# Scores tied behind the first MoE's matmuls, maxima in other PSUM banks, and one step less of lag, in a fused attention and two-MoE kernel

## The chip, the cores and the metric

The kernel runs on one core of a Trainium2 chip. The metric is the device time of one execution in microseconds (us), as a median over runs. Five engines work side by side, each on its own queue of instructions in a fixed order: TensorE (PE in the profile, its weight loads PEld), VectorE (DVE), ScalarE (ACT), GpSimd (POOL) and SyncE (SP), which here issues nearly all DMAs. The order in each queue is fixed when the program is built: a scheduler walks the instructions as they were written down, keeps a simulated clock, and gives each engine, whenever it is free on that clock, the earliest written instruction whose inputs and buffers are ready. On the chip an engine then works through its queue in that order and waits where an input is late.

## The reference, cut to what matters

```python
# attention: batch 4, heads 8, seq 576, head_dim 64
q_rot, k_rot = rotate(q), rotate(k)
scores = 1 / np.sqrt(D) * np.matmul(q_rot, k_rot.transpose(0, 1, 3, 2))
scores = scores - np.max(scores, axis=-1, keepdims=True)
attn = np.exp(scores)
attn = attn / (np.sum(attn, axis=-1, keepdims=True) + 1e-09)
x = np.matmul(attn, v)                       # then (B * S, H * D) = (2304, 512)
# first MoE: d_model 512, d_ff 768
h = np.maximum(np.maximum(x @ w1, x @ w2), x @ w3)
y = h @ w_out
# second MoE: d_model 512, d_ff 2048
h = y @ w_in
return (h * (1 / (1 + np.exp(-h)))) @ w_out2
```

## The kernel before, in words

**The attention** is cut into 80 tiles (`tiles`, filled from `order`, line 580). Four batches follow each other; each batch has a first part of its queries (256 columns, tiles 0 and 1 of each of four pairs of heads, 8 tiles in all) and a second part (320 columns, tiles 2, 3 and 4, 12 tiles; tile 4 is half as wide and takes both heads at once). Counted from 0, batch 1 is tiles 20 to 39, batch 2 tiles 40 to 59, batch 3 tiles 60 to 79. `attention()` (line 607) is a generator that writes down one step for each tile. In step j it writes the scores of tile j (`tile_scores`, lines 416, 417, 423 and 426, into the one tile `s` of three PSUM banks), their row maxima (`tile_max`, DVE, line 436) and exponentials (ACT, line 443). Then it writes later work on earlier tiles: the division of tile j-1 by its sums (`tile_norm`, ACT, line 455), and for batches 1 to 3 (`moved(b)`) a DMA that moves its 32-row blocks (`tile_move`, SP, line 494); for tile j-2 a transposition of the last columns through TensorE (`tile_last`, line 505; `turn_last`, lines 461 and 462); for tile j-3 a 32x32 transposition on DVE of what the DMA brought (`tile_flip`, line 516); then attention times V for a finished part of a pair (`av`, lines 557 and 561, its result read by ACT, line 564, and DVE, line 565). `av_at` says at which step a part's `av` is written: the index after its last tile plus 2, plus 1 for batches 1 to 3.

**The first MoE** runs inside the attention. Its work is cut into groups: an up group is 12 matmuls of one output block for one of w1, w2, w3, a down group 18 (`group`, line 640, matmuls on line 649). A batch has 36 up groups (18 on 256 columns for the first part, 18 on 320 for the second) and 8 down groups. From batch 1 on the first three up groups of the second part are written ahead of the first part's down groups. An up group's result is read by ACT (line 665, for w1) or by DVE (line 667, for w2 and w3), a down group's by ACT (line 691). While the attention lasts, groups write into `ps_m`, a ring of two PSUM banks, so the third group needs the first one's bank to be read. After each step the main loop at the end of `fused_kernel` gives groups out: `debt` grows by `RATE`, 8,000 columns, up to 24,000, and groups are written as long as it is positive, a group costing its columns times its matmuls (3,072 or 3,840 for an up group), and as long as the step has reached `x_ready` of the group's batch and part. So two or three up groups stand between two steps, none where the next part's x isn't there yet. With `x_ready[1, 1]` at 45 and `x_ready[2, 1]` at 65, steps 42 to 44 and step 64 give out none. Batch 3's groups start with one a step from step 77 on, and the rest follows when the attention is over, with five more banks (`ps_g`) in place of the attention's.

**Maxima over partitions** scale the fp16 pairs into which weights and activations are split. `all_max_a` (line 120 on PE, 122 on DVE) turns a column of maxima on TensorE and reduces it, `all_max_b` (line 128) spreads the result over the partitions, and `scale_of` (from line 143) reads it. Each takes a bank from `max_bank()` (line 114): a bank of `ps_m`, the ring of the groups. After tile 26 these are the maxima of V for batches 2 and 3, of `w_in` and of the second `w_out`.

**The turns.** `ps_t`, a ring of two banks with the tag `tr`, holds what TensorE transposes for the attention: q and k (`qk_turn`, lines 373 and 387) and the last columns of each tile (lines 461, 462 and 505).

**Beside all this** the weights of the second MoE are prepared (ACT lines 153, 227, 921, DVE lines 238, 239, 925, POOL lines 229 and 917, DMAs of SP), and after the attention come the rest of batch 3 and the second MoE (lines 1044 to 1139).

`tc.issue_after(x)` makes what is written inside it stand behind instruction `x` in the queue of x's engine. It sets the order alone and adds no wait.

Of the kernel before, what the change touches and what calls it, by code (L numbers as in the profile page):

```python
# [7 lines left out]
F32 = mybir.dt.float32  # L8
# [9 lines left out]
P = 128  # L18
# [4 lines left out]
def fused_kernel(  # L23
# [22 lines left out]
    nc = tc.nc  # L46
    B, H, S, D = q.shape
    NP = H // 2
# [26 lines left out]
    ps_m = Ring(ctx, "ps_m", 2, space=PSUM)  # L75
# [19 lines left out]
    ps_t = Ring(attn_pools, "ps_t", 2, space=PSUM)  # L95
# [13 lines left out]
    zscr = {nm: dram.tile([P, KC * (F2 // 512) * 512], F32, name="z" + nm) for nm in ("wi", "wo")}  # L109


    ps_am = []

    def max_bank():
        return (ps_am[0] if ps_am else ps_m).tile([P, 512], F32, tag="m", name="m")

    def all_max_a(m, ps=None):

        ps = ps or max_bank()
        nc.tensor.transpose(ps[0:1, 0:P], m, ident)  # L120
        t = small.tile([1, 1], F32, tag="amax", name="amax")
        nc.vector.tensor_reduce(out=t, in_=ps[0:1, 0:P], op=ALU.max, axis=AX.X)
        return t
# [147 lines left out]
    last = {}  # L271
# [87 lines left out]
    def moved(b):  # L359
        return b > 0  # L360
# [45 lines left out]
    def both(s, o, step, n):  # L406

        return bass.AP(tensor=s.tensor, offset=s.offset + o, ap=[list(s.ap[0]), [step, 2], [1, n]])
    evacs = [0]

    def tile_scores(key):
        b, hp, t = key
        T, K, Q = T_t[b, hp]
        s = ps_s.tile([P, 1536], F32, tag="s", name="s")
        if t == 4:
            nc.tensor.matmul(s[:, 0:512], Q, T[:, 512:1024], start=True, stop=True)
            last["score"] = nc.tensor.matmul(s[:, 512:576], Q, T[:, 1024:1088], start=True, stop=True).ins
            s_t[key] = s
            return
        n = P  # L420
        qs = T[:, t * P:t * P + n]
        kt = T[:, 512:1024]
        nc.tensor.matmul(both(s, 512, 448, 64), qs, K, start=True, stop=True)
        for g, o in ((0, 0), (1, 1024)):
            r = slice(64 * g, 64 * g + 64)
            last["s"] = last["score"] = nc.tensor.matmul(s[:, o:o + 512], qs[r], kt[r], start=True, stop=True).ins  # L426
        s_t[key] = s
# [4 lines left out]
    def tile_max(key):  # L432
        s = s_t.pop(key)
        m = heads(key)
        nb = small.tile([P, 2], F32, tag="nb", name="nb")
        x = nc.vector.tensor_reduce(  # L436
            out=nb[:, 0:m], in_=both(s, 0, 960, 576) if m > 1 else s[:, 0:576], op=ALU.max, axis=AX.X, negate=True
        )
        last["max"] = x.ins
        e = e_p.tile([P, 1152], F32, tag="e", name="e")  # L440
        sm = small.tile([P, 2], F32, tag="sm", name="sm")
        for g in range(m):
            x = nc.scalar.activation(  # L443
                out=e[:, HK[g]], in_=s[:, SK[g]], func=AF.Exp, bias=nb[:, g:g + 1], accum_out=sm[:, g:g + 1]
            )
        exps.append(x.ins)
        e_t[key], sum_t[key] = e, sm

    def tile_norm(key):
        e, m = e_t[key], heads(key)  # L450
        r = small.tile([P, 2], F32, tag="rec", name="rec")
        nc.scalar.activation(out=r[:, 0:m], in_=sum_t.pop(key)[:, 0:m], func=AF.Copy, bias=1e-9)
        nc.vector.reciprocal(out=r[:, 0:m], in_=r[:, 0:m])  # L453
        for g in range(m):
            nc.scalar.activation(out=e[:, HK[g]], in_=e[:, HK[g]], func=AF.Copy, scale=r[:, g:g + 1])  # L455
# [12 lines left out]
    def pt_of(key):  # L468
        b, hp, t = key
        r = int(t > 1)  # L470
        if (b, hp, r) not in pt_t:
            pt_t[b, hp, r] = pt_p.tile([P, 9, PARTS[r][1]], F32, tag="pt", name="pt")
        return pt_t[b, hp, r], P * t - PARTS[r][0]

    def blocks(pt):

        w = pt.shape[2]
        f = pt.rearrange("p c w -> p (c w)")
        return f[:, 0:8 * w].rearrange("p (i c k) -> p i c k", c=8, k=32), f[:, 8 * w:9 * w]

    def tile_move(key):

        e = e_t[key]
        pt, o = pt_of(key)
        main, i = blocks(pt)[0], o // 32
        for j in range(4):
            r = slice(32 * j, 32 * j + 32)
            if key[2] == 4:
                of = e[:, 128 * j:128 * j + 128]
                to = main[r, i:i + 2].rearrange("p i (g c) k -> p (i g) (c k)", g=2)  # L490
            else:
                of = bass.AP(tensor=e.tensor, offset=e.offset + 128 * j, ap=[list(e.ap[0]), [640, 2], [1, 128]])
                to = main[r, i:i + 4].rearrange("p i (g c) k -> p i g (c k)", g=2)
            nc.sync.dma_start(out=to, in_=of)
# [15 lines left out]
    def tile_flip(key):  # L510

        pt, o = pt_of(key)
        n = 2 if key[2] == 4 else 4
        x = blocks(pt)[0][:, o // 32:o // 32 + n].rearrange("p i c k -> p (i c k)")
        with tc.issue_after(last["max"]):
            nc.vector.transpose(out=x, in_=x)  # L516
# [28 lines left out]
    def av(b, hp, r):  # L545
        if hp == 0 and r == 0:
            x_t[b] = x_p[b % 2].tile([P, NP * S], F32, tag="x", name="x").bitcast(F16).rearrange("p (a x s) -> p a x s", a=NP, x=2)
        pt, vv = pt_t.pop((b, hp, r)), v_t[b, hp]
        o, n = PARTS[r][:2]
        v4 = vv[:, 0:4, :].rearrange("p a x -> p (a x)").rearrange("p (h c d) -> p h c d", h=2, c=4)  # L550
        xp = ps_x.tile([P, 512], F32, tag="xp", name="xp")
        if moved(b):
            main, mixed = blocks(pt)
            turned = lambda c, g: main[:, :, c + 4 * g, :]
        else:
            mixed, turned = pt[:, 4, :], lambda c, g: pt[:, c + 5 * g, :]
        nc.tensor.matmul(xp[:, 0:n], vv[:, 4, :], mixed, start=True, stop=False)
        for c in range(4):
            for g in range(2):
                r = slice(64 * g, 64 * g + 64)  # L560
                nc.tensor.matmul(xp[r, 0:n], v4[:, g, c, :], turned(c, g), start=False, stop=(c == 3))  # L561
        xh, xl = x_t[b][:, hp, 0, o:o + n], x_t[b][:, hp, 1, o:o + n]
        sv = sv_t[b][0]
        nc.scalar.activation(out=xh, in_=xp[:, 0:n], func=AF.Copy, scale=sv)
        nc.vector.scalar_tensor_tensor(
            out=xl, in0=xp[:, 0:n], scalar=sv, in1=xh, op0=ALU.mult, op1=ALU.subtract
        )
# [5 lines left out]
    PARTS = [(0, 256, (0, 1)), (256, 320, (2, 3, 4))]  # L573
    order = [(b, hp, r) for b in range(B) for r in range(2) for hp in range(NP)]
    tiles, events, first, x_ready, av_at = [], {}, {}, {}, {}

    def at(j, f, *a):
        events.setdefault(j, []).append((f, a))

    for b, hp, r in order:  # L580
        first.setdefault((b, hp), len(tiles))
        tiles += [(b, hp, t) for t in PARTS[r][2]]
        av_at.setdefault(len(tiles) + 2 + moved(b), []).append((b, hp, r))
        x_ready[b, r] = len(tiles) + 4 + moved(b)
    for i, (b, hp) in enumerate(pairs):
        u = first[b, hp]
        if b > 1:
            j = first[b, 0] + 3 * hp - 7
# [10 lines left out]
    for b in range(1, B):  # L599
# [4 lines left out]
        at(u, v_scale, b)  # L604
        at(u + 1, v_scale_b, b)

    def attention():

        back = lambda j, n: tiles[j - n] if n <= j < len(tiles) + n else None
        for j in range(len(tiles) + 5):  # L610
            if j < len(tiles):
                tile_scores(tiles[j])
                tile_max(tiles[j])
            key = back(j, 3)
            if key and moved(key[0]):
                tile_flip(key)
            for a in av_at.pop(j, ()):
                av(*a)
            key = back(j, 1)
            if key:  # L620
                tile_norm(key)
                if moved(key[0]):
                    tile_move(key)
            key = back(j, 2)
            if key:
                (tile_last if moved(key[0]) else tile_turn)(key)
            for f, a in events.pop(j, ()):
                f(*a)
            yield
# [11 lines left out]
    def group(passes, n, ps=None, more=False):  # L641

        first = ps is None
        if first:
            wide_n[0] += 1
            ring, tag = (ps_g[0], "mg") if ps_g and wide_n[0] % 7 > 1 else (ps_m, "m")
            ps = ring.tile([P, 512], F32, tag=tag, name=tag)
        for i, (l, r) in enumerate(passes):
            nc.tensor.matmul(ps[:, 0:n], l, r, start=(first and i == 0), stop=(not more and i == len(passes) - 1))  # L649
        return ps  # L650

    def moe1(b, pools):
# [672 lines left out]
        pass  # L1325
    for _ in wprep4:
        pass
    attn_pools.close()
    tail = ExitStack()
    ps_g.append(Ring(tail, "ps_g", 5, space=PSUM))  # L1330
# [82 lines left out]
```

## Time and profile before

| | |
|---|---|
| three runs: median, lowest, highest | 1001.32, 1000.82, 1008.92 us |
| the profiled execution, its span | 1006.66 us, 1004.8 us |
| mean granted clock of TensorE | 0.969 of full speed |
| busy share: PE, DVE, ACT, POOL | 92%, 70%, 60%, 49% |
| tile 26 starts, tile 79 starts, last attention matmul ends | 194.6, 576.4, 597.0 us |

The profile is of one execution, and its times are us from the start of its span. The span is shorter than the execution by what lies around it, 1.9 us here. PE, DVE, ACT, POOL are the busy times of the engines; a granted clock of 1.00 is 2.4 GHz, one of 0.50 is 1.2 GHz. An arrow <- behind an idle time names what ended it.

### The profile page before, as it was taken

To read this page: it belongs to the slowest core of one execution; us is meant where nothing else is said; L and a number is where in the kernel's file an instruction comes from. 1 tells how busy PE (TensorE), PEld (TensorE's weight loads), DVE (VectorE), ACT (ScalarE), POOL (GpSimd) and SP (SyncE) were. 2 spreads that over 40 slices of the span, in tenths; PEclk is the share of its full clock that TensorE was granted. 3 is DMA by queue.
4 is the path that set the end of the run, shared out by engine and by line. 5 is a ranking of instruction groups with operands and counts; after the bars stand their busy time and mean duration, and the time that the engine had idled before them with its cause. 6 is when DMAs were issued, how large, how long until landed. Compare 5 with 4: busy or idle time off the path is not lost. (4 is left out here: it accounts for less than half of the span.)

```text
span 1004.8 us, 19162 instructions
## 1 busy us (share of the span) xinstructions
PE 922.8 (92%) x6802; PEld 674.3 (67%) x6802; DVE 698.6 (70%) x1231; ACT 604.4 (60%) x1381; POOL 490.9 (49%) x546
## 2 busy tenths in 40 slices
PE   4577999999999899998998989999998999999997
PEld 2344665555666556665655567788887888888886
DVE  5779877967578556897767546854778767856554
ACT  2888577757667656787867623653563544554442
POOL 5835594961455500633322205653678259255264
PEclk9798999999999899999998999999999999999999
DMA  6943135877788965789988846264454253333201
GB/s 150 295 118 104 34 100 120 190 143 161 165 180 191 183 107 96 203 225 228 215 212 188 205 115 212 72 189 147 134 188 132 74 174 102 114 122 125 66 1 42
DMA packets 185198, 146.29 MB, mean 146 GB/s; under 512 B 51216, under 2 KB 168720, under 8 KB 185104
## 3 DMA queue, kind: packets, MB, share of 16 engines
q1 hardware_dynamic: 183600, 144.36, 56.5%
q8 instruction: 54, 0.88, 0.4%
q10 hardware_dynamic: 1504, 0.72, 0.3%
q14 instruction: 40, 0.33, 0.1%
HBM read 90.51 MB, written 26.21 MB: 116 GB/s over the span
## 5 line engine op out<-in xcount | busy, mean ns | idle before, releaser
L649 PEld LDWEIGHTS <-w 128*128 128x128 f16 x1632 | 161.5, 100 | 70.7 <-issue 24.5
L649 PE MATMUL m<-x,w 128*128 128x256 f16 (+1 forms) x1388 | 195.4, 292 | 13.1 <-ACT t L665 6.0
L1139 PEld LDWEIGHTS <-g 128*128 128x128 f16 x1485 | 146.2, 98 | 17.6
L1076 PEld LDWEIGHTS <-w8s 128*128 128x128 f16 x1344 | 131.1, 98 | 16.1 <-issue 1.0
L436 DVE TENSOR_REDUCE nb<-s 128x2 f32<-128x1152 f32 (+1 forms) x80 | 98.7, 1233 | 42.0 <-PE s L426 38.1
L443 ACT ACTIVATE e<-s,nb 128x576 f32<-128x576 f32 x144 | 105.3, 737 | 35.2 <-DVE nb L436 33.0
L917 POOL TENSOR_TENSOR z<-z 128x128 f32<-128x128 f32 (+1 forms) x96 | 60.8, 652 | 127.7 <-DMA z<-zwi 49.4
L229 POOL TENSOR_SCALAR z<-z 128x256 uint16<-128x256 uint16 x64 | 52.9, 826 | 123.0 <-ACT z L227 77.7
L455 ACT ACTIVATE e<-e,rec 128x576 f32<-128x576 f32 x144 | 104.5, 768 | 12.9 <-DVE rec L453 12.4
L426 PE MATMUL s<-T 64*128 64x512 f32 x256 | 85.9, 707 | 0.0
L561 PE MATMUL xp<-pt,vd 128*64 128x256 f32 (+1 forms) x512 | 81.5, 416 | 2.7 <-DVE pt L516 2.7
L1090 POOL TENSOR_TENSOR z<-t 128x256 f32<-128x256 f32 x32 | 27.1, 847 | 89.0 <-DVE t L1082 54.0
L516 DVE STREAM_TRANSPOSE pt<-pt 128x1024 f32<-128x1024 f32 (+1 forms) x60 | 67.6, 1127 | 2.8 <-DMA pt<-e 2.8
L1028 DVE SCALAR_TENSOR_TENSOR g<-gsum,sg,g 128x1024 f16<-128x1024 f32 x36 | 49.1, 1372 | 23.5 <-ACT g L1027 23.1
L352 POOL TENSOR_TENSOR w<-qk,sin_sb 128x512 f32<-128x512 f32 (+2 forms) x44 | 45.0, 1044 | 40.7 <-DMA qk<-in_q_dram 37.5
L649 PE MATMUL m<-h,wo 128*128 128x256 f16 (+1 forms) x448 | 63.2, 291 | 0.0
L1027 ACT ACTIVATE g<-gsum,sg 128x1024 f16<-128x1024 f32 x36 | 40.9, 1143 | 36.5 <-POOL gsum L1023 36.5
L649 PEld LDWEIGHTS <-wo 128*128 128x128 f16 x512 | 50.3, 100 | 17.2 <-issue 2.7
L561 PEld LDWEIGHTS xp<-pt,vd 128*64 128x64 f32 x512 | 35.9, 136 | 37.6 <-issue 13.4
L239 DVE SCALAR_TENSOR_TENSOR z<-z,z 128x256 int32<-128x256 int32 x64 | 36.3, 567 | 20.2 <-POOL z L229 19.0
L667 DVE SCALAR_TENSOR_TENSOR t<-m,t 128x256 f32<-128x256 f32 (+1 forms) x82 | 36.8, 449 | 18.5 <-PE m L649 15.7
L1139 PE MATMUL c<-w,g 128*128 128x256 f16 x376 | 48.9, 277 | 0.0
(246 smaller groups left out, 1970.7 us busy)
## 6 DMA issues: line engine op xcount, KB each, us to landing
w8s<-w8scr SPq DMA_DIRECT2D x64, 448.0 KB, 4.4
pt<-e SPq DMA_DIRECT2D x192, 128.0 KB, 4.0
z<-in_moe_w_in_dram SPq DMA_DIRECT2D x32, 256.0 KB, 3.9
z<-in_moe_w_out_dram SPq DMA_DIRECT2D x32, 256.0 KB, 3.7
w<-in_moe_w_dram SPq DMA_DIRECT2D x6, 768.0 KB, 5.2
wo<-in_moe_w_dram SPq DMA_DIRECT2D x6, 768.0 KB, 4.6
qk<-in_q_dram SPq DMA_DIRECT2D x32, 128.0 KB, 3.2
vd<-in_v_dram SPq DMA_DIRECT2D x16, 256.0 KB, 3.1
```

What stands on the lines that cost most here:

```text
L229: nc.gpsimd.tensor_scalar(out=q[:, :, 2], in0=q[:, :, 1], scalar1=step, scalar2=off, op0=ALU.mult, op1=ALU.add)
L426: last["s"] = last["score"] = nc.tensor.matmul(s[:, o:o + 512], qs[r], kt[r], start=True, stop=True).ins
L436: x = nc.vector.tensor_reduce(out=nb[:, 0:m], in_=both(s, 0, 960, 576) if m > 1 else s[:, 0:576], op=ALU.max, axis=AX.X, negate=True)
L443: x = nc.scalar.activation(out=e[:, HK[g]], in_=s[:, SK[g]], func=AF.Exp, bias=nb[:, g:g + 1], accum_out=sm[:, g:g + 1])
L455: nc.scalar.activation(out=e[:, HK[g]], in_=e[:, HK[g]], func=AF.Copy, scale=r[:, g:g + 1])
L516: nc.vector.transpose(out=x, in_=x)
L561: nc.tensor.matmul(xp[r, 0:n], v4[:, g, c, :], turned(c, g), start=False, stop=(c == 3))
L649: nc.tensor.matmul(ps[:, 0:n], l, r, start=(first and i == 0), stop=(not more and i == len(passes) - 1))
L917: nc.gpsimd.tensor_tensor(out=z[:, o], in0=z[:, x], in1=z[:, y], op=op)
L1028: nc.vector.scalar_tensor_tensor(out=l, in0=x, scalar=sg_t[jb], in1=h, op0=ALU.mult, op1=ALU.subtract)
L1076: nc.tensor.matmul(o, l, r, start=(i == 0), stop=(i == len(passes) - 1))
L1139: x = nc.tensor.matmul(ps, l, r, start=first, stop=last_, skip_group_check=True)
```

## The change

There are three edits.

- `group` keeps its last matmul in `last["group"]`, and from step 26 on (`j > LOOSE`) `tile_scores` is written inside `tc.issue_after(last["group"])`: the three or two score matmuls of tile j stand in TensorE's queue behind every group that was given out before step j.
- From step 26 on until the attention and the preparations that follow it have been written, `max_bank()` takes its bank from `ps_t` (tag `tr`) instead of `ps_m`.
- For the second part of batch 3 the extra step falls away: `tile_flip` of its 12 tiles is written 2 steps behind the scores instead of 3, and `av` and `x_ready` come one step earlier.

```diff
--- before.py
+++ after.py
@@ -109,10 +109,11 @@
     zscr = {nm: dram.tile([P, KC * (F2 // 512) * 512], F32, name="z" + nm) for nm in ("wi", "wo")}
 
 
-    ps_am = []
+    ps_am, b_now = [], [0]
 
     def max_bank():
-        return (ps_am[0] if ps_am else ps_m).tile([P, 512], F32, tag="m", name="m")
+        ring, tag = (ps_am[0], "m") if ps_am else (ps_t, "tr") if b_now[0] else (ps_m, "m")
+        return ring.tile([P, 512], F32, tag=tag, name=tag)
 
     def all_max_a(m, ps=None):
 
@@ -580,8 +581,9 @@
     for b, hp, r in order:
         first.setdefault((b, hp), len(tiles))
         tiles += [(b, hp, t) for t in PARTS[r][2]]
-        av_at.setdefault(len(tiles) + 2 + moved(b), []).append((b, hp, r))
-        x_ready[b, r] = len(tiles) + 4 + moved(b)
+        lag = int(moved(b) and (b, r) != (B - 1, 1))
+        av_at.setdefault(len(tiles) + 2 + lag, []).append((b, hp, r))
+        x_ready[b, r] = len(tiles) + 4 + lag
     for i, (b, hp) in enumerate(pairs):
         u = first[b, hp]
         if b > 1:
@@ -604,16 +606,22 @@
         at(u, v_scale, b)
         at(u + 1, v_scale_b, b)
 
+    LOOSE = 25
+    LAST = [(B - 1, hp, t) for hp in range(NP) for t in PARTS[1][2]]
+
     def attention():
 
         back = lambda j, n: tiles[j - n] if n <= j < len(tiles) + n else None
         for j in range(len(tiles) + 5):
+            b_now[0] = int(j > LOOSE)
             if j < len(tiles):
-                tile_scores(tiles[j])
+                with tc.issue_after(last["group"]) if j > LOOSE else nullcontext():
+                    tile_scores(tiles[j])
                 tile_max(tiles[j])
-            key = back(j, 3)
-            if key and moved(key[0]):
-                tile_flip(key)
+            for n in (3, 2):
+                key = back(j, n)
+                if key and moved(key[0]) and n == 3 - (key in LAST):
+                    tile_flip(key)
             for a in av_at.pop(j, ()):
                 av(*a)
             key = back(j, 1)
@@ -646,7 +654,8 @@
             ring, tag = (ps_g[0], "mg") if ps_g and wide_n[0] % 7 > 1 else (ps_m, "m")
             ps = ring.tile([P, 512], F32, tag=tag, name=tag)
         for i, (l, r) in enumerate(passes):
-            nc.tensor.matmul(ps[:, 0:n], l, r, start=(first and i == 0), stop=(not more and i == len(passes) - 1))
+            x = nc.tensor.matmul(ps[:, 0:n], l, r, start=(first and i == 0), stop=(not more and i == len(passes) - 1))
+        last["group"] = x.ins
         return ps
 
     def moe1(b, pools):
@@ -1325,6 +1334,7 @@
         pass
     for _ in wprep4:
         pass
+    b_now[0] = 0
     attn_pools.close()
     tail = ExitStack()
     ps_g.append(Ring(tail, "ps_g", 5, space=PSUM))
```

## Rows read from the trace of the kernel before

**Rows 1.** The page: span, and the granted clock in 40 slices.

```profile
span 1004.8 us, 19162 instructions
PEclk9798999999999899999998999999999999999999
```

**Rows 2.** Busy time by stage: length, PE, PEld, DVE, ACT, POOL, clock, DMA.

```profile
194.50:333.00 138.50, 131.12 (x831) 82.23 (x831) 100.47 (x176) 90.88 (x262) 73.89 (x80) 0.96 0.82 172
333.00:439.00 106.00, 102.38 (x655) 64.92 (x654) 71.14 (x128) 71.86 (x192) 29.16 (x37) 0.97 0.75 153
439.00:577.00 138.00, 125.73 (x790) 77.62 (x791) 97.54 (x189) 102.20 (x282) 41.85 (x71) 0.96 0.89 210
577.00:612.00 35.00, 31.50 (x243) 23.70 (x243) 15.65 (x39) 10.26 (x28) 2.31 (x4) 0.95 0.61 183
612.00:1004.80 392.80, 382.58 (x3409) 333.94 (x3406) 262.63 (x434) 192.05 (x293) 218.27 (x230) 0.99 0.36 113
```

**Rows 3.** Who waited for whom, PE, 194.5 to 612: us in total, times, longest.

```profile
PE s L423 <- ACT e L443: 5.9, 6, 2.1
PE s L416 <- ACT e L443: 5.7, 2, 3.6
PE m L649 <- ACT t L665: 4.0, 5, 1.4
PE m L649 <- DVE t L667: 3.5, 1, 3.5
PE m L649 <- DVE swie L143: 0.2, 1, 0.2
```

**Rows 4.** Busy time by stage, line 649 alone: PE (x matmuls), PEld, clock, DMA.

```profile
0.00:194.50 194.50, 41.77 (x312) 29.82 (x312) 0.93 0.51 137
194.50:304.90 110.40, 57.66 (x420) 41.73 (x420) 0.95 0.79 167
304.90:332.50 27.60, 12.59 (x96) 9.47 (x96) 1.00 0.92 187
332.50:409.30 76.80, 43.94 (x306) 30.65 (x306) 0.96 0.72 125
```

**Rows 5.** Busy time by stage, all instructions: four stretches, columns as in rows 2.

```profile
304.90:332.50 27.60, 25.68 (x173) 16.39 (x173) 22.14 (x43) 20.72 (x61) 20.01 (x22) 1.00 0.92 187
409.30:438.90 29.60, 29.11 (x200) 19.57 (x198) 26.28 (x47) 25.41 (x72) 15.93 (x21) 1.00 0.85 231
341.90:348.70 6.80, 6.64 (x25) 3.79 (x26) 3.63 (x6) 5.13 (x16) 1.19 (x2) 0.50 0.94 178
529.70:536.40 6.70, 5.76 (x18) 3.39 (x19) 5.58 (x13) 5.52 (x17) 3.09 (x6) 0.50 0.76 126
```

**Rows 6.** Timeline: start, us, engine, line, operation, count [idle before <-releaser].

```profile
530.64 2.07 PE L416 MATMUL s<-T,qd 128*128 128x512 f32 x2 [3.60 <-ACT e L443]
...
548.14 3.42 PE L649 MATMUL m<-x,w 128*128 128x320 f16 x24
...
570.86 0.38 PE L423 MATMUL s<-kd,T 128*128 128x128 f32 x2
...
574.75 0.74 ACT L443 ACTIVATE e<-s,nb 128x576 f32<-128x576 f32 x1
...
576.39 1.02 PE L416 MATMUL s<-T,qd 128*128 128x512 f32 x2
```

**Rows 7.** Timeline, 582 to 588: the end of the attention.

```profile
585.42 1.25 DVE L516 STREAM_TRANSPOSE pt<-pt 128x1024 f32<-128x1024 f32 x1 [2.81 <-DMA pt<-e]
...
587.11 1.17 PE L649 MATMUL m<-x,w 128*128 128x256 f16 x7 [3.50 <-DVE t L667]
```

**Rows 8.** Timeline, 444 to 448: a maximum over partitions.

```profile
444.29 0.27 PE L120 MATMUL m<-ident,vm 128*1 128x128 f32 x1
...
445.80 0.27 DVE L122 TENSOR_REDUCE amax<-m 1x1 f32<-1x128 f32 x1
```

**Rows 9.** DMA issues of the page: KB each, us from issue to landing.

```profile
pt<-e SPq DMA_DIRECT2D x192, 128.0 KB, 4.0
```

## The prediction

> **What bounds the kernel now.** I read the page's span and clock line first, then the busy times by stage, then who waited for whom on TensorE, and last the matmuls of line 649 counted by stretch. From the scores of tile 26 at 194.5 us to the end of the attention TensorE is busy 131.1 of 138.5, 102.4 of 106.0, 125.7 of 138.0 and 31.5 of 35.0 us [rows 2]. It is the bound, and 26.8 us of this stage are its idle time. The granted clock is below full here too: 138.5 x 0.04 + 106 x 0.03 + 138 x 0.04 + 35 x 0.05 = 16.0 us of full-speed time [rows 2], the lower digits in the clock line of the page [rows 1]. The matmuls themselves stay the same in number and shape. So about 43 us are all that the tie and the bank edit can win or share out anew; after 612 us TensorE has 382.6 of 392.8 us of work [rows 2], which the change does not touch.
>
> Which waits are they? Scores that wait for the exponentials of the tile before, 5.9 + 5.7 = 11.6 us in 8 waits; groups that wait for their bank or input, 4.0 + 3.5 us [rows 3]; the rest is spread over turns and `av`. The longest score wait, 3.60 us, is followed by score matmuls of 2.07 us, where the same two take 1.02 us at full clock [rows 6]: the stretch behind it ran 6.7 us at 0.50, and 6.8 us at 0.50 stand behind the 2.1 us wait at tile 46 [rows 3, 5]. That is (6.7 + 6.8) / 2 = 6.75 us more.
>
> **The tie: what it changes in the order.** Counting by the planner (8,000 columns a step, 3,072 or 3,840 a group), 396 matmuls of groups have been given out before step 26: 288 of batch 0's first half and 60 + 24 + 24 of its second. TensorE had issued 312 when the scores of tile 26 began [rows 4]: 84 behind, seven groups. At tile 41 the count is 792 given out (all 576 of batch 0, 216 of batch 1) against 312 + 420 = 732: 60 behind. At tile 55 it is 1134 against 312 + 420 + 96 + 306 = 1134 [rows 4]: none. So from tile 26 to about 54, and again from 60 to 77 (48 behind at tile 73), the edit changes the queue; between 55 and 59 the order is already the tied one.
>
> **Its gain.** Where the scores waited for exponentials, groups stood behind them with their data ready: two groups of 320 columns last 3.42 us [rows 6], enough for 2.1 and nearly for 3.60 us. Tied, such groups stand in front. At most this wins all of 11.6 + 6.75 = 18.4 us; at least nothing, since the mean number of groups between two scores stays the same and a late exponential can meet a thin step. I take half, -9.2 us, because the order is fixed by a planned time: before, scores were placed as soon as the plan had the exponentials done, with no margin, and tied they can only come later relative to the groups.
>
> **Its cost.** The stock of 24 to 84 matmuls is gone. Steps 42 to 44 and 64 give out nothing. From tile 41 to 45 the stock did 96 matmuls, 12.59 of 25.68 us of work [rows 4, 5]; without them 13.1 us are left for four steps, 3.3 us each. A step cannot be shorter than the chain from scores to the end of the second exponential, 570.86 to 575.49, 4.6 us [rows 6]. So an empty step idles 1.3 us. At step 44 the next part's first groups already have most of their x, so I count 42, 43 and 64: +4.0 us (0 to 5.2). Then the banks: before, groups came in pairs, one for each of the two banks (24 in one row [rows 6]). Tied, the 15 steps from 26 on that give out 36 or more matmuls have a third group in front of the scores, which needs the first one's bank read by ACT or DVE, behind their exponentials or maxima. The longest wait for such a read by ACT was 1.4 us [rows 3]. I take one such wait, +1.4, since two groups in a row already run without one; the ends are 0 and 15 x 1.4 = 21 us. A scores matmul queued behind a waiting group also holds the maximum and exponentials of its tile, which is part of these 21. Tie in all: -9.2 + 4.0 + 1.4 = -3.8 us.
>
> Here a rule speaks against the change. In rows 5 both stretches at 0.50 stand behind waits of scores, and the 1.4 us bank wait is shorter than either of those. The Trainium skill, TensorE: Matmul & The Clock Gate, section "A second HAM failure mode: psum-queue depth-cycling", says that matmul groups which cycle through PSUM banks leave small idle times between them, which can make the clock swing between its two levels and cost throughput. By the row the sum above stands; by the rule each of the 15 bank waits would bring a half-speed stretch too, which is the last rival below.
>
> **The maxima.** Four maxima after tile 26 take eight banks. One holds its bank from 444.29 to 446.07 us, 1.8 us [rows 8]. Groups waited openly for this only 0.2 us [rows 3]; the gain is at most the 4.0 + 0.2 us of waits for a free bank, at least nothing. In the turns' ring the same holds can delay a transposition: if half of the eight meet one for half their length, 8 x 1.8 / 4 = 3.6 us. I take -0.5, near the 0.2.
>
> **The lag.** Twelve DVE transpositions are written one step earlier. A step is 382 / 53 = 7.2 us. The DMA lands 4.0 us after its issue [rows 9], so a flip two steps behind its scores has about 14.4 - 7.2 - 4.0 = 3.2 us for the division and the issue between: in time, with little to spare, and nothing gained while other groups fill TensorE. At the end of the attention a flip waited 2.81 us for its DMA, a read of a group's bank stood behind it on DVE, and TensorE idled 3.50 us [rows 7]; with the slow clock of that stage, 35 x 0.05 = 1.75, this is 5.25 us. Writing the flip earlier does not land the DMA earlier, but it may move other work in front. I take a quarter, -1.3; the ends are -5.25 and three new waits of 2.81, +8.4. The earlier `av` frees nothing: the second part's groups of batch 3 come behind its first part's in any case.
>
> **Sum.** -3.8 - 0.5 - 1.3 = -5.6 us. The profiled execution took 1006.66 us, 1.9 more than its span [rows 1]; it would become 1001.1. It lies 5.3 us above the median of the three runs, 1001.32, so the median becomes 995.7, say 996.
>
> **Rivals.**
> *The stage becomes dense.* From 409.3 to 438.9 us, where nothing is behind and the order is already the tied one, TensorE is busy 29.11 of 29.6 us at clock 1.00 [rows 5], 1.7% idle. Over 194.5 to 577 us idle and clock cost 23.3 + 14.2 = 37.5 us; at 1.7% of 382.5 they would cost 6.5. Against it: from 439 on ACT is busy 102 and DVE 98 of 138 us [rows 2], and their delays stay. With two thirds of the 31 us: 1001.3 - 20 = 981. Chance 0.2.
> *The tie does not matter.* Waits of scores turn into waits of groups for the same late ACT and DVE work, one for one. For it: the mean work between two scores is unchanged. Against it: the half-speed stretches come behind score waits alone. 1001, chance 0.21.
> *Two banks are too few (slower).* In front of the scores each third group waits 1.4 us, 15 times: 21 + 4.0 - 9.2 - 1.8 = +14, 1015. It decides from 9.2 + 1.8 - 4.0 = 7.0 us of such waits on, five of them. For it: the stock was there because groups were being held back. Against it: only 4.0 us of such waits before. Chance 0.14.
> *The same with the clock.* If every such wait also brings 3.4 us at half speed, half of a stretch like those of rows 5, 15 x 1.7 = 25 us more: 1040. By the psum-queue rule of the page named above; the rows show such stretches behind longer waits only. Chance 0.03.
>
> **How the numbers follow.** My forecast, 996 with its own range 990 to 1002, has 0.42. A measurement of this kernel tells about 1%, 10 us, from no change. Faster by more than that, below 991.3: the dense case, 0.20, and a fifth of my forecast's, 0.09, so 0.29. Slower, above 1011.3: most of the two bank cases, 0.14. Within 1%: 0.57. The range 979 to 1014 leaves out the far half of the dense case's own spread and the far part of the bank cases, some 0.2 in all.
>
> **What would show it.** Right: after tile 26 the matmuls of line 649 issued at each score equal those given out; waits of scores for exponentials fall to about half of 11.6 us; fewer stretches at 0.50; idle of one to two us at tiles 42, 43 and 64; maxima on `tr`. Wrong: waits of line 649 for reads on line 665 or 667 of over 12 us in all, new waits of line 516 for its DMA before tile 77, or idle time of TensorE between 194 and 612 us outside 15 to 30 us.

## The result, and the profile after

The kernel after takes 990.87 us in the median of 4 runs (990.28 to 993.84), the kernel before 1003.09 us in runs beside it: a ratio of 0.9881, 95% interval 0.9853 to 0.9909, or 11.9 us less. I had forecast 996, 5.6 us less, with the time most likely within 1% (0.57). The measured 1.2% is the faster case, to which I gave 0.29. The range holds the result because it is wide; the size is half of what came, and the cause that I named is not the one.

The page of the kernel after, its span and clock line [rows 1], and the group of the DVE transpositions:

```profile
span 988.7 us, 19152 instructions
...
PEclk9599899999999999989999899999999999999999
...
L517 DVE STREAM_TRANSPOSE pt<-pt 128x1024 f32<-128x1024 f32 (+1 forms) x60 | 67.7, 1128 | 11.8 <-DMA pt<-e 11.8
```

Line numbers are each kernel's own: here those after 114 are one higher as far as 583, line 649 is 657, and those after it are nine higher. To see where the time came from, take the whole stage in which the edits act, from 194.5 us to the last matmul of the first MoE: the same 2865 matmuls in both. The busy times by stage, first the kernel before, cut that way, and what follows the stage:

```profile
194.50:659.40 464.90, 436.60 (x2865) 282.66 (x2866) 321.19 (x588) 298.24 (x796) 175.00 (x219) 0.97 0.75 171
659.40:1004.80 345.40, 336.71 (x3059) 299.76 (x3057) 226.25 (x373) 169.01 (x258) 190.48 (x201) 0.99 0.37 117
```

And the kernel after:

```profile
194.50:645.30 450.80, 419.15 (x2865) 277.87 (x2866) 320.38 (x590) 299.56 (x798) 175.22 (x220) 0.98 0.79 176
645.30:988.70 343.40, 335.10 (x3059) 298.81 (x3057) 226.84 (x373) 168.54 (x258) 190.28 (x201) 1.00 0.37 118
```

The stage is 14.1 us shorter. TensorE's idle time did not shrink: 464.9 - 436.6 = 28.3 us before, 450.8 - 419.15 = 31.65 us after. Its busy time did, by 17.45 us, with the same matmuls. A part of that is the clock (0.97 and 0.98 in the column), but not most of it. The other 2.0 us, behind the stage, are mostly a stretch at half speed that this execution of before had at 778.8 us and the other had not.

Who waited for whom on TensorE, kernel after, 194.5 to 645.3 us [rows 3]:

```profile
PE s L424 <- ACT e L444: 9.1, 4, 5.5
PE m L657 <- DVE t L676: 6.3, 4, 2.3
PE xp L562 <- DVE pt L517: 5.3, 2, 3.8
PE m L657 <- ACT t L674: 2.8, 2, 2.1
PE s L417 <- ACT e L444: 2.7, 3, 2.1
```

Scores wait 9.1 + 2.7 = 11.8 us for exponentials, where they waited 11.6. So in this kernel the waits that I had the tie remove are all still there.

**What became shorter** is seen in the groups of TensorE's instructions, shapes kept apart. Kernel before, same stage; line 426 is the two head matmuls of a tile, 561 `av`:

```profile
L426 PE MATMUL s<-T 64*128 64x512 f32 x168 | 55.2, 669 | 0.0
L561 PE MATMUL xp<-pt,vd 128*64 128x320 f32 x192 | 35.6, 445 | 2.0 <-DVE pt L516 2.0
...
L561 PE MATMUL xp<-pt,vd 128*64 128x256 f32 x176 | 24.2, 387 | 0.7 <-DVE pt L516 0.7
```

Kernel after:

```profile
L427 PE MATMUL s<-T 64*128 64x512 f32 x168 | 50.1, 675 | 0.0
...
L562 PE MATMUL xp<-pt,vd 128*64 128x320 f32 x192 | 32.2, 441 | 0.1
...
L562 PE MATMUL xp<-pt,vd 128*64 128x256 f32 x176 | 23.0, 399 | 5.3 <-DVE pt L517 5.3
```

The mean duration of one hardly moved (669 and 675 ns), but the time that the 168 cover together fell from 55.2 to 50.1 us: more of them ran at the same time. The three groups together cover 5.1 + 3.4 + 1.2 = 9.7 us less. The timeline of the kernel before shows how. Each head's scores need 64 of the array's 128 rows, and a matmul on f32 stands as two records, so a tile's two heads are x4:

```profile
203.80 1.12 PE L426 MATMUL s<-T 64*128 64x512 f32 x2
204.86 3.43 PE L649 MATMUL m<-x,w 128*128 128x320 f16 x24
208.22 1.12 PE L426 MATMUL s<-T 64*128 64x512 f32 x2
...
213.44 1.13 PE L426 MATMUL s<-T 64*128 64x512 f32 x4
```

Side by side in the queue, both heads take 1.13 us. With two groups between them each takes 1.12 us alone. The groups stood there because they were late: in the scheduler's order a group written earlier goes first as soon as its bank is free, even between two matmuls of one tile. The same happened to the eight half-array matmuls of `av` (64 columns each). The Trainium skill, TensorEngine Tiling (Array Packing), section "Key Properties", says that tiles of the array which don't overlap can run matmuls in parallel; the rows agree, and add that a full-array matmul between the two ends it.

In the queue of before 5 of the 42 two-head tiles from tile 26 on have their heads apart, in that of after none; the last 20 `av` parts, from batch 1's second part on (the expectations below call them "from batch 1 on"), had come in 36 runs and now come in 26. Of the five pairs, three have 22 to 24 matmuls between their heads, nearly all of groups, the others four matmuls and a single transposition.

### The profile page after: what moved, and what is told of

The parts are those of the page before. It is cut to its first block, busy times and chain, and to the rows that moved or that the text cites. A ratio compares the mean times of both kernels' runs of the same rounds, so it can differ in the third digit from the quotient of the medians.

```text
span 988.7 us, 19152 instructions
## 1 busy us (share of the span) xinstructions
PE 903.3 (91%) x6802; PEld 669.0 (68%) x6802; DVE 698.5 (71%) x1231; ACT 605.1 (61%) x1381; POOL 490.5 (50%) x546
## 5 line engine op out<-in xcount | busy, mean ns | idle before, releaser
L657 PE MATMUL m<-x,w 128*128 128x256 f16 (+1 forms) x1388 | 192.9, 288 | 14.5 <-DVE t L676 6.3
L1085 PEld LDWEIGHTS <-w8s 128*128 128x128 f16 x1344 | 131.1, 98 | 16.1 <-issue 0.9
L456 ACT ACTIVATE e<-e,rec 128x576 f32<-128x576 f32 x144 | 104.1, 768 | 11.8 <-DVE rec L454 11.2
L562 PE MATMUL xp<-pt,vd 128*64 128x256 f32 (+1 forms) x512 | 76.9, 418 | 5.4 <-DVE pt L517 5.3
L427 PE MATMUL s<-T 64*128 64x512 f32 x256 | 78.8, 695 | 0.0
L517 DVE STREAM_TRANSPOSE pt<-pt 128x1024 f32<-128x1024 f32 (+1 forms) x60 | 67.7, 1128 | 11.8 <-DMA pt<-e 11.8
L562 PEld LDWEIGHTS xp<-pt,vd 128*64 128x64 f32 x512 | 35.6, 137 | 39.3 <-issue 11.9
L1148 PE MATMUL b<-w,g 128*128 128x256 f16 x376 | 48.5, 273 | 0.0
L1148 PE MATMUL a<-w,g 128*128 128x256 f16 x376 | 47.9, 273 | 0.0
```

The source lines that it names most:

```text
L657: x = nc.tensor.matmul(ps[:, 0:n], l, r, start=(first and i == 0), stop=(not more and i == len(passes) - 1))
L1085: nc.tensor.matmul(o, l, r, start=(i == 0), stop=(i == len(passes) - 1))
L1148: x = nc.tensor.matmul(ps, l, r, start=first, stop=last_, skip_group_check=True)
```

## The experiments

Each is timed against the kernel before on the same chip; not all ran on the same chip, so kernels are compared by these ratios. Theory A: the gain is such pairs kept together. Theory C is my prediction's: groups in front of scores save waits and half-speed stretches. Theories B, D and E ask which edit it is. In the names, "whole" means pairs kept together by high priority, "apart" pairs split, and what else stands there is the edits that are in.

In the table, "work" is worked out from the traces for the stage above: the time by which each matmul moves the end of TensorE's work on, less half of what of it lies in a half-speed stretch. Idle is the stage's length less the busy time of its window. With the clock loss, the other half of the half-speed time, the three add up to the stage within 1 us. Of the 11.1 us of work between before and after, the head matmuls are 5.2 and the half-array matmuls of `av` 4.4.

| kernel | ratio to before, 95% interval | heads apart | av runs | work | idle | clock loss |
|---|---|---|---|---|---|---|
| before | 1 | 5 | 36 | 422.1 | 28.3 | 14.8 |
| before, second profile | | 5 | 36 | 422.1 | 31.6 | 8.0 |
| after | 0.9881 (0.9853 to 0.9909) | 0 | 26 | 411.0 | 31.7 | 8.6 |
| tie_only | 0.9971 (0.9947 to 0.9994) | 0 | 27 | 413.4 | 35.7 | 7.1 |
| max_only | 0.9916 (0.9885 to 0.9946) | 3 | 34 | 418.5 | 24.6 | 9.3 |
| lag_only | 0.9947 (0.9918 to 0.9975) | 4 | 34 | 419.8 | 29.6 | 11.0 |
| no_tie (maxima and lag) | 0.9932 (0.9902 to 0.9961) | 3 | 33 | 417.8 | 31.3 | 6.7 |
| tie_max | 0.9896 (0.9872 to 0.9921) | 0 | 27 | 411.8 | 29.8 | 7.9 |
| whole_no_tie | 0.9897 (0.9866 to 0.9929) | 0 | 20 | 406.0 | 32.7 | 8.5 |
| whole_max_lag | 0.9844 (0.9811 to 0.9877) | 0 | 20 | 408.1 | 30.5 | 7.2 |
| whole_max | 0.9808 (0.9781 to 0.9836) | 0 | 20 | 407.3 | 27.7 | 8.4 |
| all_whole | 0.9948 (0.9924 to 0.9972) | 0 | 20 | 408.8 | 34.4 | 7.3 |
| apart | one run, 1009.22 us | 42 | 26 | 456.4 | 10.0 | 1.7 |

**The unchanged kernel a second time.** 

> The kernel before, unchanged, for a second profile. The same queue must give the same work of TensorE at full clock in the stage (422.1 us) within 1 us, whatever theory holds. If idle and half-speed time of the stage (28.3 and 14.8 us in the first profile) differ by several us here, differences of that size between single profiles say nothing, and only work at full clock and the timed medians are to be compared.

The work is the same to 0.1 us, while the clock loss fell from 14.8 to 8.0 us and the idle time rose by 3.3. The second profile's stage:

```profile
194.50:656.20 461.70, 430.13 (x2867) 280.28 (x2867) 319.08 (x588) 296.66 (x796) 175.24 (x219) 0.98 0.75 172
```

Its waits in that stage:

```profile
PE m L649 <- ACT t L665: 6.2, 3, 2.4
PE s L416 <- ACT e L443: 6.1, 3, 3.6
PE s L423 <- ACT e L443: 6.0, 6, 2.0
PE m L649 <- DVE t L667: 5.2, 2, 3.5
```

Scores wait 12.1 us here, as before, but groups wait 6.2 + 5.2 = 11.4 us for reads of their banks, where the first profile had 4.0 + 3.5 = 7.5 [rows 3].

So half-speed stretches cost 7 us more or less between executions of one queue. The 16.0 us of them that my prediction hoped to lower by reordering were partly chance of that one execution, and differences of single profiles in these two columns carry little below; even a named wait can differ by 4 us between two profiles of one queue.

**Which edit.**

The tie alone:

```diff
             if j < len(tiles):
-                tile_scores(tiles[j])
+                with tc.issue_after(last["group"]) if j > LOOSE else nullcontext():
+                    tile_scores(tiles[j])
```

> The kernel before with the tie alone; maxima and lag stay. In its queue no two-head tile after tile 26 has its two half-array score matmuls apart (before: 5 of 42) and the av parts from batch 1 on come in 27 runs (before 36, after 26). Theory A (the tie wins by keeping half-array matmuls side by side, where two run at once, and by fewer half-speed stretches): 9 to 13 us faster than before, within 3 us of the kernel after. Theory B (the other two edits bring the gain): within 3 us of before.

Measured 2.9 us faster (0.6 to 5.3 by the interval): not A's 9 to 13, and within B's 3. But its work fell by 8.7 us, as A has it. What took much of it back, as far as one profile tells, stands in its waits, 194.5 to 650:

```profile
PE m L652 <- DVE amax L122: 6.3, 2, 3.5
PE m L652 <- ACT t L669: 5.6, 3, 3.9
PE s L423 <- ACT e L443: 5.3, 5, 2.0
PE m L652 <- DVE t L671: 3.5, 2, 2.3
PE m L652 <- DVE ve L143: 3.5, 2, 2.1
...
PE s L416 <- ACT e L443: 2.2, 4, 1.2
```

Groups now wait 6.3 + 3.5 = 9.8 us for a bank of `ps_m` that a maximum of V holds. Before, the scheduler let scores and other work pass meanwhile, and the price stayed hidden in the order. Tied, scores stand behind the held group. The scores' own waits for exponentials, 5.3 + 2.2 = 7.5 us, are shorter here than in either profile of before (11.6 and 12.1), so in this run the tie did what my prediction wanted of it.

Maxima and lag without the tie:

```diff
-                with tc.issue_after(last["group"]) if j > LOOSE else nullcontext():
-                    tile_scores(tiles[j])
+                tile_scores(tiles[j])
```

> The kernel after without the tie: maxima in the turns' banks and the shorter lag alone. 3 of 42 two-head tiles are apart, av comes in 33 runs. Theory A: (5 - 3) x 1.1 + (36 - 33) x 0.4 = 3.4 us less work on TensorE, so 0 to 6 us faster than before. Theory B: 9 to 13 us faster, as the kernel after.

Measured 6.8 us faster: above A's 3.4 and just outside its 0 to 6, below B's 9; its interval, 3.9 to 9.8, touches both. So neither edit alone explains the whole, and the two halves were run further.

Tie and maxima, with the old lag: 

> The kernel after with the old lag: tie and maxima. The tie alone left groups waiting 6.3 + 3.5 us for the bank that a maximum held. Theory D (tie and maxima belong together: the tie shortens TensorE's work but puts groups, and so the scores behind them, behind the held banks): those waits are gone, 9 to 13 us faster than before. Theory E (the maxima add nothing to the tie; the rest of the gain is the shorter lag): 2 to 5 us faster, as the tie alone.

10.4 us faster, as D's numbers have it and outside E's. The waits of groups for maxima are gone from its trace, and it is within the intervals the kernel after: the shorter lag adds nothing measurable to these two (0.9896 and 0.9881).

The maxima alone:

```diff
     def max_bank():
-        return (ps_am[0] if ps_am else ps_m).tile([P, 512], F32, tag="m", name="m")
+        ring, tag = (ps_am[0], "m") if ps_am else (ps_t, "tr") if b_now[0] else (ps_m, "m")
+        return ring.tile([P, 512], F32, tag=tag, name=tag)
```

> The kernel before with the maxima in the turns' banks alone. In its queue groups are no longer behind from tile 53 on (0 to 18 in place of 36 to 66 at tiles 64 to 70), 3 of 42 two-head tiles are apart, av comes in 34 runs. Theory D: 3 to 8 us faster, most of what maxima and lag gave together (6.8 us). Theory E: within 2 us of before.

8.4 us faster: above D's range, far from E. This edit too reorders the queue: with two banks left to the groups they catch up, 18 or fewer behind at tiles 65 to 70 where before had 36 to 66, and no tie was needed for it. 3.6 us of the 8.4 are work (two heads and two `av` breaks fewer); the rest is idle and clock time, which single profiles can't settle. By itself this edit is the largest of the three, and it adds to the tie almost in full: 2.9 + 8.4 = 11.3 us apart, 10.4 together. So D's "belong together" is not shown; each is worth about the same without the other. Nor were the held banks all that took the tie's gain back: with the maxima moved, the tie saves 6.7 us of work (418.5 to 411.8) and idle time rises by 5.2 (24.6 to 29.8).

The lag alone:

```diff
-        av_at.setdefault(len(tiles) + 2 + moved(b), []).append((b, hp, r))
+        lag = int(moved(b) and (b, r) != (B - 1, 1))
+        av_at.setdefault(len(tiles) + 2 + lag, []).append((b, hp, r))
```

> The kernel before with the shorter lag of the last part alone. The queue up to tile 76 is nearly that of before, 4 of 42 two-head tiles are apart, av comes in 34 runs. Theory D: within 3 us of before (my prediction's own term was -1.3). Theory E: 4 to 8 us faster.

5.3 us faster, against D's 3 and inside E's range. 2.3 us of it are work. The edits don't add up, 2.9 + 8.4 + 5.3 = 16.6 us apart and 11.9 together, and that is the lag's doing: maxima and lag are 8.4 + 5.3 us apart and 6.8 together. They remove some of the same breaks, but that explains only a part: of work they save 3.6 + 2.3 us apart and 4.3 together.

**Pairs together without any of the edits.**

```diff
-            last["s"] = last["score"] = nc.tensor.matmul(s[:, o:o + 512], qs[r], kt[r], start=True, stop=True).ins
+            with tc.high_priority():
+                last["s"] = last["score"] = nc.tensor.matmul(s[:, o:o + 512], qs[r], kt[r], start=True, stop=True).ins
...
-                nc.tensor.matmul(xp[r, 0:n], v4[:, g, c, :], turned(c, g), start=False, stop=(c == 3))
+                with tc.high_priority():
+                    nc.tensor.matmul(xp[r, 0:n], v4[:, g, c, :], turned(c, g), start=False, stop=(c == 3))
```

> The kernel before, with the two head matmuls of a tile and the eight half-array matmuls of an av part written at high priority, so that a group no longer comes between them; no tie, maxima and lag as before. Groups still lag: 48 to 84 matmuls behind at tiles 26 to 33 and 63 to 75. No two-head tile is apart, av comes in 20 runs from batch 1 on. Theory A, its first half (side by side): 5 x 1.1 + 16 x 0.4 = 12 us less work on TensorE, 8 to 14 us faster than before. Theory C (what counts is that groups stand in front of scores, so that scores wait less and the clock stays up; my prediction's reason): within 4 us of before, since the lag is still there.

10.3 us faster: A, and against C, since at tiles 26 to 33 and 65 to 75 the groups are about as far behind as before. In between they are less so (at tile 41 none, before 60): high priority also moves `av` and scores forward in the queue, so this run alone doesn't separate the two theories fully. Its stage:

```profile
194.50:641.80 447.30, 414.57 (x2862) 276.51 (x2859) 318.99 (x588) 298.42 (x796) 174.60 (x219) 0.98 0.76 176
```

447.3 - 414.6 = 32.7 us idle, no less than in either profile of before; only the busy time fell. The work fell by 16.1 us, more than the 12 that A counted and more than the 10.3 that the time did.

**Pairs apart on purpose.** The block-diagonal score matmul goes between the heads of each tile from tile 26 on:

```diff
-        nc.tensor.matmul(both(s, 512, 448, 64), qs, K, start=True, stop=True)
         for g, o in ((0, 0), (1, 1024)):
             r = slice(64 * g, 64 * g + 64)
             last["s"] = last["score"] = nc.tensor.matmul(s[:, o:o + 512], qs[r], kt[r], start=True, stop=True).ins
+            if not g:
+                nc.tensor.matmul(both(s, 512, 448, 64), qs, K, start=True, stop=True)
...
```

(Shortened: the order of the three is fixed with `issue_after`, and tiles before 26 are left as they were.)

> The kernel after, with the block-diagonal score matmul placed between the two head matmuls from tile 26 on: the same matmuls, all 42 pairs apart. Theory A: each pair takes 2 x 1.12 us in place of 1.13, so TensorE's score work grows by 42 x 1.1 = 46 us and the time by 25 to 46 us. Theory C: the order of three matmuls of one tile costs nothing, within 4 us of the kernel after.

The first pair in its timeline, the head matmuls' group and the stage of this run:

```profile
205.36 1.12 PE L429 MATMUL s<-T 64*128 64x512 f32 x2
206.41 0.49 PE L432 MATMUL s<-kd,T 128*128 128x128 f32 x2
206.83 1.12 PE L429 MATMUL s<-T 64*128 64x512 f32 x2
```

```profile
L429 PE MATMUL s<-T 64*128 64x512 f32 x168 | 94.7, 643 | 2.8 <-ACT e L449 2.7
```

```profile
194.50:662.50 468.00, 457.99 (x2856) 286.02 (x2855) 322.02 (x587) 302.10 (x796) 174.62 (x218) 1.00 0.74 168
```

94.7 - 50.1 = 44.6 us more of TensorE's time for the same 168 records, as A said (46), nearly a doubling. The time grew by only 18 us over the kernel after (20 when each is taken against before on its own chip; this is one run), below A's 25: idle time fell from 31.65 to 468.0 - 458.0 = 10.0 us, and the clock is 1.00. Most exponentials were done when TensorE came back for them: scores wait 3.2 us for them in place of 11.8. So idle time of the bound engine was a cushion here, and the work added moved the time by less than its size.

**The tie with the pairs together in both.** 

> The kernel after without the tie, with the head matmuls and the half-array matmuls of av at high priority instead, so that no group comes between them. No two-head tile apart, av in 20 runs (after 26), groups 12 to 36 behind the scores at tiles 60 to 75. Theory A's first half (side by side is what the tie is worth): the 10.3 us of the high priority alone and the maxima's waits on top, 12 to 17 us faster than before, 1 to 5 us faster than the kernel after. Theory C (groups in front of scores are what counts): slower than the kernel after, 3 to 10 us faster than before.

15.6 us faster than before, as A says, against C.

> The kernel after, all three edits, with the head matmuls and av's half-array matmuls at high priority as well. Beside the run without the tie it differs by the tie alone, and in both every pair stays together (no two-head tile apart, av in 20 runs): what is left is the place of the scores relative to the groups. Theory A (the tie's worth was the pairs): no faster than that run without the tie (15.6 us faster than before), 10 to 16 us faster than before. Theory C (groups in front of scores save waits and half-speed stretches): 3 to 8 us faster than that run, 18 to 24 us faster than before.

Only 5.2 us faster than before: with the pairs kept by other means, adding the tie costs some 10 us (intervals 0.9811 to 0.9877 and 0.9924 to 0.9972). The waits of the run with the tie, 194.5 to 650:

```profile
PE s L424 <- ACT e L445: 14.6, 10, 4.9
PE m L659 <- ACT t L676: 6.3, 3, 5.0
```

and of the run without it:

```profile
PE s L424 <- ACT e L445: 9.9, 7, 4.7
...
PE m L658 <- ACT t L675: 2.0, 1, 2.0
```

Scores wait more, not less, when tied, 14.6 against 9.9 us, and groups wait more for their banks, 6.3 against 2.0. This is the reverse of the tie's gain in my prediction, and its cost there in kind. But the profile with the tie is of its fastest execution, 990.39 us where the median is 995.59, and only 3.4 us above the other profile's 987.03. So these waits are a sign, and where the 10 us between the medians go is not shown.

**The lag with the pairs together.** 

> Maxima in the turns' banks and pairs at high priority, without the tie and with the old lag: beside the run that has the shorter lag too it differs by the lag alone, with every pair together in both. If the lag's 5.3 us when it was alone came from TensorE's work (one split pair and two av breaks fewer, 2.3 us of work), nothing of it is left here: within 2 us of the run with the shorter lag, some 15 us faster than before. If the earlier av of the last part is worth something of its own, this run is 3 to 6 us slower than that one, 10 to 12 us faster than before.

18 us faster by its medians (0.9808), the fastest of all, and no slower than with the shorter lag (0.9844; the intervals overlap, 0.9811 to 0.9836). It is 2.5 to 3.6 us beyond that run, so a little outside the 2 us expected, on the side away from the other case. So the earlier `av` is worth nothing of its own here, and what the lag alone gave goes with the changed order as far as these runs show. Its stage has little work and little idle time together, 443.0 - 415.3 = 27.7 us:

```profile
194.50:637.50 443.00, 415.28 (x2865) 277.31 (x2866) 323.96 (x592) 299.42 (x803) 177.02 (x221) 0.98 0.77 179
```

## Why the prediction was right and wrong

**The first step was wrong.** "The matmuls themselves stay the same in number and shape. So about 43 us are all that the tie and the bank edit can win or share out anew." The matmuls stayed the same, but not their time: 422.1 to 411.0 us at full clock, 11.1 us less, beside 11.9 us in the time. I took TensorE's busy time as given and looked only at idle time and clock. The rows that would have told were in the trace: x2 in 1.12 us and x4 in 1.13 us on the same line.

**The tie's gain (-9.2) named the wrong cause.** That groups stood late behind the scores, 84 matmuls at tile 26, was counted rightly, and after the change the issued matmuls equal those given out at tile 26 (396) or run ahead. But score waits went from 11.6 to 11.8 us. With the tie alone they did fall, to 7.5; with the maxima in place they rose with it (8.2 to 9.9), with maxima and lag too (9.7 to 11.8), and so they did with the pairs kept together. So fewer score waits are no steady effect of the tie. What it does in every run where the pairs aren't kept otherwise is that no late group cuts a pair of half-array score matmuls.

A reading behind this term was too narrow as well: half-speed stretches do not stand behind score waits alone. In the profile that I read, those at 195.1 and 277.0 us stand behind a turn's wait of 2.05 us and an `av`'s of 2.02, the one at 447.7 behind waits of 1.13 (scores) and 0.43 us (a bank), and the one at 587.6 behind the 3.50 us for a bank [rows 7].

**Its costs are not told apart from chance.** From tile 41 to 45, now 304.5 to 338 us, TensorE is busy 25.73 us, as before in 27.6 [rows 5]:

```profile
304.50:338.00 33.50, 25.73 (x161) 15.40 (x160) 21.28 (x40) 22.50 (x64) 25.83 (x30) 0.95 0.96 198
```

7.8 us idle against 1.9, where I had 4.0 for these steps and step 64. But between the same tiles the second profile of before idles 31.1 - 27.3 = 3.8 us and the tie alone 28.0 - 25.4 = 2.6, so the cost of the empty steps does not show in the tie by itself. Bank waits after the change are 6.3 + 2.8 = 9.1 us; I had forecast a rise of 1.4, and the two profiles of before, 7.5 and 11.4, lie on both sides. The tie's sum, -3.8, is close to the 2.9 us measured for it alone, but by luck, through two errors against each other: 8.7 us of work not seen, and idle time not seen, with 9.8 us of waits for the maxima's bank in that profile.

**The maxima (-0.5) were mis-sized, outside my bounds of -4.2 to +3.6:** 8.4 us alone, and some 7.5 on top of the tie (0.9971 to 0.9896). I sized the edit by the open wait of 0.2 us. A wait that the scheduler has already worked around need not show as a wait: with the edit the count of matmuls behind at tiles 65 to 70 fell from 36 to 66 to 18 or fewer. How much of the gain that is stays open.

**The lag (-1.3)** had 5.3 us alone, where it removed breaks, and nothing measurable behind the other edits. Its risk was the one I named: the DVE transpositions wait 11.8 us for their DMAs, 2.8 before [rows 7], and 5.6 of them lie before tile 77.

**The rivals.** The dense stage did not come: idle time did not fall. "The tie does not matter" has the waits right and the time wrong. The slower case with two banks has the direction of what the tie does once the pairs are kept together, 10 us, but that bank waits are its cause is not shown. The swings of the clock by the Trainium skill's rule in the last rival did not come: 20.5 us of half speed in the stage after, 30.7 and 17.1 us in the two profiles of before.

**The signs.** After the change all groups given out stand in front of the scores, as I wrote. Score waits did not halve. Two signs of being wrong came: the transpositions' waits before tile 77, and 417.5 - 385.85 = 31.65 us idle between 194.5 and 612 us, above 30. The second says little, since the second profile of before has 31.6 there too.

Left open: how much of the 4.8 us that the maxima won beyond their work is idle time and how much chance of the clock, why the lag alone won 3 us more than its work, and where the tie's 10 us go when the pairs are together. Keeping the pairs together and tying fewer steps was not tried.

## What to carry to other kernels

Where two matmuls each use half of the array, count in the queue how often something stands between them: busy time hides it, and the group's covered time over its count and mean shows it. Keep such pairs together directly (here by priority, 10.3 us, and 18 with the maxima's banks moved) rather than by an ordering that also holds other work up. A bank ring shared by a rare slow user can cost more than its open waits: here moving that user to another ring won 8.4 us where 0.2 us of waits stood open.

## What was not expected of the hardware

A full-array matmul between two half-array ones ended their overlap even where it was as short as 0.49 us, and splitting all 42 pairs took 44.6 us of TensorE's time but some 18 us of the kernel's. In a pair of the kernel before a transposition of 0.33 us did the same, 2.43 us for both heads. The half-speed stretches of the same queue summed to 30.7 us in one execution's stage and 17.1 us in another's.
